# Weighting the first half of the positions in four groups of 128 instead of three, in a local attention and S4 kernel on one Trainium2 core

## The chip, the core and the metric

The kernel runs on one core of one Trainium2 chip. The core has five engines that work at the same time, each in the order of its own queue: TensorE (PE: matrix products, PEld its weight loads), VectorE (DVE), ScalarE (ACT), GpSimd (POOL) and SyncE (SP, which here only issues transfers). Matrix products land in PSUM, a small accumulator memory of eight banks, and are copied from there to SBUF, the working memory, by ScalarE or VectorE. Transfers between SBUF and the chip's main memory are issued from SP, POOL and ACT. The metric is the time of one execution in microseconds; less is better. Three runs of the kernel before gave 405.63, 408.08 and 410.88 us.

## The reference

Two independent layers read their own inputs, and their outputs stand side by side in one array of 2048 rows and 1280 columns.

```python
# A: attention over 8 positions, 2 apart, 32 heads of 20 dimensions
qkv = (x @ wqkv)                       # x: 2048 x 640
logits[h, s, w] = q[h, s] . k[h, s - 2 w] * 20 ** -0.5     # w = 0..7, -1e9 where s - 2 w < 0
attn = softmax(logits over w)
o[h, s] = sum over w of attn[h, s, w] * v[h, s - 2 w]
a = o @ wo
# B: state-space layer, as a long convolution
K[d, l] = Re(sum over n of C * exp(dt * A * l) * dt * B)   # 640 x 192 states, l < 2048
y = irfft(rfft(u padded) * rfft(K padded)) + u * Dskip     # along the 2048 positions
out = concat(a, y)
```

## The kernel before

Layer B is computed first: the kernel K from tables of exponentials and sines, then transforms along the positions as matrix products. Its spectra go to main memory (Zdram, UDdram) and come back at the end for the last inverse step. Layer A's projections of keys and queries, its logits and the first softmax lie between and behind these. The change touches only the last stage, from about 317 us of the profiled execution on.

The 2048 positions are held as four segments of 512 (one per 32 partitions: partition 32 s + h is head h of segment s). "First half" means positions 0 to 255 of each segment, "second half" positions 256 to 511; each half has its own softmax (arguments 0 and 1 of `softmax_a`, `exp`, `sums`, `reciprocal`, `softmax_b`). The first half's weights are ready before the stage begins; the second half's softmax is finished inside it.

**Values.** `proj_v(d)` projects two of the 20 value dimensions, d and d+1, for all positions: 40 matrix products into one two-bank PSUM buffer, and one copy by ScalarE into the tile v. There are three such two-bank buffers, shared by everything that asks for one ("big"). In front of its 512 positions each segment has a halo of 14 columns, the last 14 of the segment before; `v_halo(d0, nd)` fills it for nd dimensions with four small products and one ScalarE copy. It reads the copied v.

**Weighting.** `av_step(i0, ni, j0, nj, w)` is one step: VectorE multiplies the values of 4 nj dimensions at ni positions, shifted by 2 w, by the weights of offset w, into one of six ring buffers (the profile calls them atp and prod); TensorE adds the result over w with 16 matrix products of 32x32 tiles (weights: ident) into two two-bank PSUM buffers ps_o. For w = 0 the shift is zero and no halo column is read. A group is the eight steps w = 0 to 7; at its end two ScalarE copies empty the two buffers. A step's number is n = 8 group + w. A ring buffer is written again six steps later, when its products are done; all groups behind the second use the same two PSUM buffers.

**Pieces.** When the positions of a group have all 20 dimensions, they can be multiplied by wo and sent out: `out_piece`, 10 matrix products of 320 columns, copies (two of 320 columns for the even pieces, one of 640 for the odd ones) and the transfers to the output. There are 16 pieces, numbered here 0 to 15 in order: 0 to 3 and 4 to 7 of the first half, 8 to 10, 11 to 13, and 14 and 15 of the second. From piece 11 on half of a piece's transfers are issued from ScalarE's own queue. `rest` is the list of pieces that may run.

**Parts.** Layer B's last inverse step is 24 parts (`part`), three for each of eight blocks of output rows: a few matrix products, one ScalarE copy (ysb), and after every third part four transfers to the output. Parts 0 to 5 read quarter 0 of the spectra, 6 to 11 quarter 1, 12 to 17 quarter 2, 18 to 23 quarter 3. Quarter 2 is loaded into the space of x (which `proj_v` reads), quarter 3 into the space of quarter 0; `LOADS` issues them at n = 2 to 6 and 8 to 12, 15 transfers of 128 KB for a quarter.

**Order.** A planner orders each engine's queue by which instruction can go first; but from `att.in_order()` on, the stage's matrix products, the copies, the VectorE steps and the output transfers of the pieces are pinned to the order in which the program writes them. `FILLS` is the table that places pieces and parts: n: (pieces, parts), run behind step n (in group 0 the parts run ahead of the step). What is left runs behind the last step.

Of the kernel before, what the change touches and what calls it, by code (L numbers as in the profile page):

```python
# [781 lines left out]
def body(tc, ctx, pools, prm, B_u, B_Dskip, Sd, Zd, UDd, A_x, A_wqkv, A_wo, out_a, out_b):  # L782
# [41 lines left out]
    att = Attention(tc, pools, A_x, A_wqkv, A_wo, out_a, psk, psg)  # L824
# [139 lines left out]
    for w in range(W):  # L964
        if w >= 2:
            att.products(1, w)
        att.logits(1, w)
        att.proj_v(2 * w)
        if w == 4:
            att.v_halo(0, 8)  # L970
    att.in_order()
    inv.open_rows()
    inv.load(1)
# [1 line left out]
    rest = []  # L975

    def fill(some, n=1):
        for f in some[0:n]:
            f()
        del some[0:n]  # L980

    att.open_out(a2)
    GROUPS = ((0, 256, 0, 2, ()), (0, 128, 2, 3, [(s, 1, 0, 128) for s in range(4)]), (128, 128, 2, 3, [(s, 1, 128, 128) for s in range(4)]),
              (256, 96, 0, 5, [(0, 4, i, 32) for i in (256, 288, 320)]), (352, 96, 0, 5, [(0, 4, i, 32) for i in (352, 384, 416)]), (448, 64, 0, 5, [(s, 2, 448, 64) for s in (0, 2)]))
    FILLS = {1: (0, 1), 3: (0, 1), 5: (0, 2), 7: (0, 2), 11: (0, 2), 13: (0, 1), 15: (0, 2), 16: (0, 1), 17: (1, 0), 19: (2, 2), 23: (1, 2), 27: (2, 2), 31: (2, 2), 35: (2, 2), 37: (0, 2), 39: (1, 0), 43: (1, 0), 45: (1, 0)}
    LOADS = {(2, 8)[n // NCH] + n % NCH: (2 + n // NCH, n % NCH) for n in range(2 * NCH)}
    for group, (i0, ni, j0, nj, done) in enumerate(GROUPS):
        for w in range(W):
            n = 8 * group + w
            if group == 0:  # L990
                if w < 7:
                    fill(parts, FILLS.get(n, (0, 0))[1])
                if w == 3:
                    att.exp(1)
                if w in (0, 3):
                    att.proj_v(16 + 2 * (w == 3))
                if w == 5:
                    att.v_halo(8, 12)
            att.av_step(i0, ni, j0, nj, w, group == 5)
            if n in LOADS:  # L1000
                qr, c = LOADS[n]
                inv.load(qr, c, c + 1)
            if n in (9, 11, 13, 14):
                k = (9, 11, 13, 14).index(n)
                att.sums(1, 2 * k, 2 * k + 2)
            if n == 2:
                att.softmax_a(1)
            if n == 17:
                att.reciprocal(1)
                att.softmax_b(1)  # L1010
            if n > 6 and n in FILLS:
                fill(rest, FILLS[n][0])
                fill(parts, FILLS[n][1])
        rest += att.out_proj(done, group == 5)
    for f in parts + rest:
        f()

# [2 lines left out]
def kernel(  # L1020
# [28 lines left out]
    Zd = dpool.tile([NCH, 128, 4096], bf16, name="Zdram")  # L1049
    UDd = dpool.tile([NCH, 128, 2048], bf16, name="UDdram")  # L1050
    body(tc, ctx, pools, prm, B_u, B_Dskip, Sd, Zd, UDd, A_x, A_wqkv, A_wo, out_a, out_b)


# [28 lines left out]
```

## Time and profile before

| | |
|---|---|
| time, median of three runs | 408.08 us (405.63 to 410.88) |
| span of the profiled execution | 400.1 us |
| VectorE busy | 363.8 us (91% of the span) |
| TensorE busy | 345.0 us (86%) |
| ScalarE busy | 308.4 us (77%) |
| weighting steps on VectorE | 335.64 to 387.89 us, 48 steps |
| last matrix product to the end of the span | 395.9 to 400.1 us |

The span runs from the first to the last instruction of one profiled execution; the times of runs also hold what lies around it, 8.0 us at the median. Rows of the timeline have the start in us, the duration in us, the engine, the line of the code, the operation, what it writes and reads, and in square brackets the idle time of the engine just before and what ended it. Several like instructions that follow each other are merged into one row with their count (x4), and its duration goes from the first one's start to the last one's end; neighbouring instructions of an engine overlap by about 0.1 us, so that the time from one start to the next is a little less than the duration. In the stage of the change the helper functions of lines 474 and 475 issue all matrix products and copies, so rows are told apart by their tiles.

### The profile page before, as it was taken

What the parts mean: (1) busy time and instruction counts of PE and PEld (TensorE: products, weight loads), DVE (VectorE), ACT (ScalarE), POOL (GpSimd) and SP (SyncE); (2) the same over time, 40 slices, a digit from 0 to 9 for tenths busy, and PEclk for the clock granted to TensorE, in tenths of its full rate; (3) what the DMA queues carried; (4) which work ended last, traced back from release to release, by engine and by line L of the source; (5) the groups of instructions that cost most, each with busy time, mean ns of one, the idle gap of its engine ahead of it and who ended that gap; (6) DMA issues with size and microseconds to landing.
All of it is one profiled execution on the core that took longest, in us unless ns stands there. A gap on an engine that the chain in (4) does not pass through costs nothing.

```text
span 400.1 us, 18758 instructions
## 1 busy us (share of the span) xinstructions
PE 345.0 (86%) x8565; PEld 258.7 (65%) x8565; DVE 363.8 (91%) x353; ACT 308.4 (77%) x536; POOL 53.5 (13%) x110
## 2 busy tenths in 40 slices
PE   1269779989998798987899999999989999888994
PEld 0157668878886677866788666656765687434652
DVE  8999998997999999979999799997967899999971
ACT  4968999889999899989999775534697554855662
POOL 8472000000010000000001000100001030032230
PEclk9997868999989899999998999999999999989999
DMA  7699103032035001440029544300563173697752
GB/s 171 155 218 188 26 3 134 31 77 61 32 136 121 14 5 57 136 106 3 3 67 206 117 100 120 100 20 3 198 177 110 52 196 78 191 238 217 232 153 81
DMA packets 41840, 43.36 MB, mean 108 GB/s; under 512 B 25409, under 2 KB 35233, under 8 KB 41121
## 3 DMA queue, kind: packets, MB, share of 16 engines
q1 hardware_dynamic: 36656, 30.19, 31.2%
q0 software_dynamic: 4208, 11.43, 9.7%
q8 instruction: 67, 1.10, 1.1%
q10 hardware_dynamic: 896, 0.54, 0.5%
q14 instruction: 13, 0.10, 0.1%
HBM read 19.70 MB, written 14.16 MB: 85 GB/s over the span
## 4 chain that ended last, share of the span: by engine, by line
PE 46%; ACT 37%; DVE 10%; issue 3%; DMA 2%; SPq 1%; ACTq 0%; DVEq 0%
ACT R L252 10%; ACT A L381 8%; ACT A L388 6%; PE ps_ph L289 5%; PE ps_q L558 5%; PE ps_k L540 4%; PE ps_k L366 4%; PE ps_k L361 4%; PE ps_v L571 4%; PE ps_f L387 3%; PE ps_x L474 3%; ACT Z L429 3%; PE ps_o L474 2%; PE ps_ia L428 2%; PE ps_l L602 2%
## 5 line engine op out<-in xcount | busy, mean ns | idle before, releaser
L348 DVE TENSOR_TENSOR Y<-PG 128x3072 bf16<-128x3072 bf16 x60 | 102.9, 1753 | 4.4 <-PE ps_k L366 4.4
L252 ACT ACTIVATE R<-LPB 128x192 bf16<-128x192 f32 (+1 forms) x185 | 56.9, 415 | 0.1
L361 PE MATMUL ps_k<-Y,X 128*32 128x64 bf16 x1920 | 47.0, 239 | 8.5 <-issue 4.2
L361 PEld LDWEIGHTS <-X 128*32 128x32 bf16 x1920 | 32.5, 117 | 18.5 <-issue 9.5
L366 PE MATMUL ps_k<-Y,X 64*32 64x64 bf16 x1920 | 42.9, 233 | 0.1
L388 ACT CAST A<-ps_f 128x1024 bf16<-128x1024 f32 x40 | 37.7, 1045 | 6.5 <-PE ps_f L387 6.5
L289 PE MATMUL ps_ph<-LPB,LPA 128*64 128x256 bf16 x320 | 33.6, 313 | 8.8 <-DMA LPA<-lo 6.6
L381 ACT CAST A<-ps_f 128x1024 bf16<-128x1024 f32 x40 | 37.7, 1031 | 2.3 <-PE ps_f L380 2.3
L318 DVE TENSOR_TENSOR X<-R,TX 128x1536 bf16<-128x1536 bf16 x40 | 37.5, 958 | 0.0
L387 PE MATMUL ps_f<-A,T 128*64 128x128 bf16 x640 | 29.7, 262 | 9.0 <-ACT A L381 8.8
L366 PEld LDWEIGHTS <-X 64*32 64x32 bf16 x1920 | 29.5, 112 | 8.4 <-issue 0.7
L387 PEld LDWEIGHTS <-T 128*64 128x64 bf16 x640 | 27.8, 132 | 10.7 <-issue 10.0
L297 ACT ACTIVATE TA<-ps_ph 128x768 bf16<-128x768 int16 x40 | 29.7, 819 | 3.6 <-PE ps_ph L293 3.5
L681 DVE TENSOR_TENSOR prod<-v,atp 128x1536 bf16<-128x1536 bf16 (+3 forms) x32 | 31.0, 1024 | 1.0 <-ACT v L475 0.5
L297 ACT ACTIVATE TX<-ps_ph 128x768 bf16<-128x768 int16 x40 | 29.7, 840 | 0.3 <-PE ps_ph L293 0.2
L591 DVE TENSOR_TENSOR prod<-qT,kT 128x1024 bf16<-128x1024 bf16 (+1 forms) x16 | 22.9, 1484 | 4.2 <-ACT qT L559 4.2
L289 PEld LDWEIGHTS <-LPA 128*64 128x64 bf16 x320 | 17.5, 122 | 13.0 <-issue 9.3
L540 PE MATMUL ps_k<-xT,wkq 128*128 128x512 bf16 x100 | 22.9, 379 | 0.2 <-ACT A L388 0.2
L293 PE MATMUL ps_ph<-LPB,LPA 128*64 128x128 bf16 x320 | 23.0, 241 | 0.0
L558 PE MATMUL ps_q<-xT,wkq 128*128 128x512 bf16 x100 | 22.6, 379 | 0.0
L318 DVE TENSOR_TENSOR PG<-R,TA 128x3072 bf16<-128x3072 bf16 x10 | 17.5, 1754 | 5.0 <-ACT TA L297 5.0
L380 PE MATMUL ps_f<-BD,U 128*64 128x128 bf16 x320 | 20.5, 286 | 0.8 <-ACT Z L429 0.6
(157 smaller groups left out, 688.5 us busy)
## 6 DMA issues: line engine op xcount, KB each, us to landing
P<-A SPq DMA_DIRECT2D x16, 256.0 KB, 3.0
Zdram<-Z SPq DMA_DIRECT2D x16, 256.0 KB, 2.4
Z<-Zdram SPq DMA_DIRECT2D x30, 128.0 KB, 4.0
U<-in_B_u_dram SPq DMA_DIRECT2D x4, 640.0 KB, 10.6
UDdram<-UD POOLq DMA_DIRECT2D x10, 256.0 KB, 3.1
out_dram<-ysb SPq DMA_DIRECT2D x32, 80.0 KB, 3.2
Z<-UDdram SPq DMA_DIRECT2D x16, 128.0 KB, 4.1
Z<-Zdram POOLq DMA_DIRECT2D x10, 128.0 KB, 5.9
```

The costliest lines, as they stand in the source:

```text
L252: exp = lambda o, i, m: nc.scalar.activation(out=o, in_=i, func=ACT.Exp, scale=m)
L289: MM(o[64 * hh:64 * hh + 64, :, 0:8], lhsT=L[:, 64 * hh:64 * hh + 64], rhs=rhs, start=first, stop=last, skip_group_check=True, tile_positi ...
L297: last = nc.scalar.activation(out=dst, in_=words.rearrange("p b (q e f) -> p b q (e f)", e=8, f=4), func=ACT.Sin, scale=PI_LO / 32768.0)
L318: TT = lambda o, a, b, op: V.tensor_tensor(out=o, in0=a, in1=b, op=op)
L348: nc.vector.tensor_tensor(out=Y[:].rearrange("p q (b a) f -> p q b a f", a=8), in0=fa, in1=gb, op=A.mult)
L361: MM(ps[32 * g:32 * g + 32, t], lhsT=X[:, q, k, :, f], rhs=Ys[k][:, q, :, f], start=(t == 0 and k == 0), stop=False, tile_position=(0, 32 ...
L366: MM(ps[32 * g:32 * g + 32, t], lhsT=X[hb, q, k, :, f], rhs=Ys[k][hb, q, :, f], start=False, stop=(k == 2), tile_position=(64 * (g // 2), ...
L381: nc.scalar.copy(out=A1[:, 8 * b:8 * b + 8], in_=ps[:])
L387: last = MM(ps[sl, kk], lhsT=C["T2"][:, 8 * b + kk, sl], rhs=A1[:, :, 8 * b + kk, :], start=(kk % 4 == 0), stop=True, skip_group_check=Tru ...
L388: nc.scalar.copy(out=A1[:, :, 8 * b:8 * b + 8, :], in_=ps[:].rearrange("p k (j g) -> p j k g", g=4))
L540: MM(ps[:, i], lhsT=self.wk[:, kt, 128 * ct:128 * ct + 128], rhs=self.x4[:, kt, 2 * i:2 * i + 2, 256 * hf:256 * hf + 256], start=(kt == 0) ...
L558: MM(ps[:, i], lhsT=self.wq[:, kt, 128 * ct:128 * ct + 128], rhs=self.x4[:, kt, 2 * i:2 * i + 2, 256 * hf:256 * hf + 256], start=(kt == 0) ...
```

## The change

The first half of the positions is weighted in four groups of eight steps instead of three, and the placing of the work around is rewritten:

- groups: 0 to 127 with dimensions 0 to 11, 0 to 127 with 12 to 19, 128 to 255 with 0 to 11, 128 to 255 with 12 to 19, where it was 0 to 255 with dimensions 0 to 7, then 0 to 127 and 128 to 255 with 8 to 19 each. The second half's three groups stay. There are 56 steps in place of 48; pieces 0 to 3 can run behind step 15 as before, 4 to 7 behind step 31 (it was 23), 8 to 10 behind 39 (31), 11 to 13 behind 47 (39);
- `proj_v(18)` goes ahead of step 1 instead of step 3; the halo is filled for dimensions 0 to 7, 8 to 11 (new, behind `proj_v(12)`) and 12 to 19 (ahead of step 3) in place of 0 to 7 and 8 to 19 (ahead of step 5);
- `FILLS` is new, and the sums of the second half's softmax are at steps 11 to 14 instead of 9, 11, 13, 14. `LOADS` and the steps behind which `softmax_a(1)`, `reciprocal(1)` and `softmax_b(1)` run (2 and 17) keep their numbers.

```diff
@@ -966,8 +966,8 @@
         att.logits(1, w)
         att.proj_v(2 * w)
-        if w == 4:
-            att.v_halo(0, 8)
+        if w in (4, 6):
+            att.v_halo(*((0, 8), (8, 4))[w // 6])
     att.in_order()
@@ -980,9 +980,11 @@
     att.open_out(a2)
-    GROUPS = ((0, 256, 0, 2, ()), (0, 128, 2, 3, [(s, 1, 0, 128) for s in range(4)]), (128, 128, 2, 3, [(s, 1, 128, 128) for s in range(4)]),
+    GROUPS = ((0, 128, 0, 3, ()), (0, 128, 3, 2, [(s, 1, 0, 128) for s in range(4)]), (128, 128, 0, 3, ()), (128, 128, 3, 2, [(s, 1, 128, 128) for s in range(4)]),
               (256, 96, 0, 5, [(0, 4, i, 32) for i in (256, 288, 320)]), (352, 96, 0, 5, [(0, 4, i, 32) for i in (352, 384, 416)]), (448, 64, 0, 5, [(s, 2, 448, 64) for s in (0, 2)]))
-    FILLS = {1: (0, 1), 3: (0, 1), 5: (0, 2), 7: (0, 2), 11: (0, 2), 13: (0, 1), 15: (0, 2), 16: (0, 1), 17: (1, 0), 19: (2, 2), 23: (1, 2), 27: (2, 2), 31: (2, 2), 35: (2, 2), 37: (0, 2), 39: (1, 0), 43: (1, 0), 45: (1, 0)}
+    END = len(GROUPS) - 1
+    FILLS = {3: (0, 1), 4: (0, 1), 5: (0, 1), 6: (0, 2), 9: (0, 2), 11: (0, 1), 15: (0, 1), 17: (1, 1), 18: (0, 1), 19: (1, 1), 21: (1, 1), 23: (1, 1), 27: (0, 2), 31: (0, 2),
+             33: (1, 0), 35: (1, 1), 37: (1, 1), 39: (1, 1), 41: (1, 1), 43: (1, 1), 45: (1, 1), 49: (1, 0), 51: (1, 0), 53: (1, 0)}
     LOADS = {(2, 8)[n // NCH] + n % NCH: (2 + n // NCH, n % NCH) for n in range(2 * NCH)}
@@ -992,16 +994,16 @@
                 if w == 3:
                     att.exp(1)
-                if w in (0, 3):
-                    att.proj_v(16 + 2 * (w == 3))
-                if w == 5:
-                    att.v_halo(8, 12)
-            att.av_step(i0, ni, j0, nj, w, group == 5)
+                if w in (0, 1):
+                    att.proj_v(16 + 2 * w)
+                if w == 3:
+                    att.v_halo(12, 8)
+            att.av_step(i0, ni, j0, nj, w, group == END)
...
-            if n in (9, 11, 13, 14):
-                k = (9, 11, 13, 14).index(n)
+            if n in (11, 12, 13, 14):
+                k = n - 11
                 att.sums(1, 2 * k, 2 * k + 2)
...
-        rest += att.out_proj(done, group == 5)
+        rest += att.out_proj(done, group == END)
     for f in parts + rest:
         f()
```

## The prediction

> **What bounds the kernel now.** I read the busy times first, then the stretches of the last stage, then VectorE's timeline there.
>
> ```profile
> PE 345.0 (86%) x8565; PEld 258.7 (65%) x8565; DVE 363.8 (91%) x353; ACT 308.4 (77%) x536; POOL 53.5 (13%) x110
> ```
>
> ```profile
> core 0: us, PE busy (x) PEld busy (x) DVE busy (x) ACT busy (x) POOL busy (x), PEclk, DMA share, GB/s
> 336.00:347.30 11.30, 10.75 (x260) 6.33 (x253) 10.69 (x12) 7.42 (x9) 0.00 (x0) 1.00 0.46 140
> ...
> 388.00:400.10 12.10, 6.92 (x106) 4.05 (x104) 1.87 (x4) 3.65 (x8) 0.00 (x0) 1.00 0.35 98
> ```
>
> No engine is the bound alone: VectorE is full from 336 to 388, TensorE nearly so (10.75 of 11.30 us in the second row), and the last 12 us belong to neither. VectorE's rows in order of time:
>
> ```profile
> 311.12 1.83 DVE L591 TENSOR_TENSOR prod<-qT,kT 128x1024 bf16<-128x1024 bf16 x3
> ...
> 335.64 2.36 DVE L681 TENSOR_TENSOR atp<-v,atp 128x2048 bf16<-128x2048 bf16 x2
> ...
> 339.05 0.42 DVE L615 TENSOR_TENSOR soft<-soft,lsb 128x512 bf16<-128x512 bf16 x1
> ...
> 340.98 3.49 DVE L681 TENSOR_TENSOR prod<-v,atp 128x2048 bf16<-128x2048 bf16 x3
> 344.38 2.35 DVE L681 TENSOR_TENSOR atp<-v,atp 128x2048 bf16<-128x2048 bf16 x2
> 347.28 3.69 DVE L681 TENSOR_TENSOR prod<-v,atp 128x1536 bf16<-128x1536 bf16 x4 [0.54 <-ACT v L475]
> ...
> 352.62 3.56 DVE L681 TENSOR_TENSOR prod<-v,atp 128x1536 bf16<-128x1536 bf16 x4
> 356.09 1.75 DVE L639 RECIPROCAL soft<-ps_x 128x256 bf16<-128x256 f32 x1
> ...
> 359.02 1.82 DVE L681 TENSOR_TENSOR atp<-v,atp 128x1536 bf16<-128x1536 bf16 x2
> ...
> 364.23 2.22 DVE L681 TENSOR_TENSOR atp<-v,atp 128x1920 bf16<-128x1920 bf16 x2
> ...
> 386.33 1.56 DVE L681 TENSOR_TENSOR prod<-v,atp 128x1280 bf16<-128x1280 bf16 x2 [0.31 <-PE ps_o L474]
> ```
>
> The first half takes VectorE from 335.64 to 364.23, and 0.54 us of that is waiting, for the copy of the last two value dimensions. The last step ends at 387.89, and then the chain of waits runs through TensorE (start, length, what):
>
> ```profile
> 365.54 0.59 PE ps_ib L474 x12
> 366.13 0.92 PE ps_o L474 x64
> 367.05 1.46 PE ps_x L474 x10
> ...
> 377.67 1.04 PE ps_o L474 x64
> ...
> 390.14 0.42 PE ps_o L474 x32
> 390.56 1.48 PE ps_x L474 x10
> 392.04 0.42 ACT ob L475
> ...
> 392.49 0.50 DVE ob L707
> ...
> 393.04 1.53 PE ps_op L474 x10
> ```
>
> TensorE ends the last step at 390.56, 2.7 us behind VectorE, runs piece 13, and waits for two copies; pieces 14 and 15 start at 393.04. What starts at 393.04 is the same after the change, so the forecast is where that start moves.
>
> **VectorE's work.** From one start to the next a step takes 3.40/3 = 1.13 us with 2048 elements (340.98 to 344.38) and 3.47/4 = 0.87 with 1536 (352.62 to 356.09): 0.52 ns an element and 0.07 us for each instruction. A step of 1024 isn't in the trace; by that line it takes 0.60, and the product of that size (first row) 1.83/3 = 0.61 at most. The first half had 8 x 1.13 + 16 x 0.87 = 23.0 us and gets 16 x 0.87 + 16 x 0.60 = 23.5: **+0.5 us**.
>
> **The values' wait.** This is the larger term. Rows of ScalarE, then of TensorE:
>
> ```profile
> 337.10 1.01 ACT L573 CAST v<-ps_v 128x1024 bf16<-128x1024 f32 x1 [1.69 <-PE ps_v L571]
> ...
> 341.96 1.01 ACT L475 CAST v<-ps_v 128x1024 bf16<-128x1024 f32 x1 [1.15 <-PE ps_v L474]
> 343.11 0.56 ACT L475 CAST ysb<-ps_ib 128x480 bf16<-128x480 f32 x1
> ...
> 344.43 1.91 ACT L626 ACTIVATE lsb<-lsb 128x2048 bf16<-128x2048 bf16 x1
> ...
> 347.93 0.31 ACT L475 CAST v<-ps_h 128x168 bf16<-128x168 f32 x1
> ...
> 354.91 1.50 ACT L475 CAST o<-ps_o 128x768 bf16<-128x768 f32 x2 [0.72 <-PE ps_o L474]
> ...
> 374.29 1.82 ACT L475 CAST ob<-ps_o 128x960 bf16<-128x960 f32 x2
> ...
> 390.84 1.15 ACTq L731 DMA_DIRECT2D out_dram<-ob  x2
> ```
>
> ```profile
> 334.71 2.33 PE L571 MATMUL ps_v<-xT,wv 128*32 128x512 bf16 x40
> 336.87 0.72 PE L602 MATMUL ps_l<-prod,wv 128*32 128x256 bf16 x20
> ...
> 341.84 0.43 PE L474 MATMUL ps_o<-atp,ident 32*32 32x512 bf16 x16
> ...
> 357.79 2.65 PE L474 MATMUL ps_op<-wo,o 128*128 128x320 bf16 x10
> ```
>
> TensorE projects values without a gap until 341.84 (2.16 us a projection, 334.71 to 336.87), while VectorE already weights. Step 0 needs no halo, so with dimensions 0 to 11 it starts at 335.64 still. Step 1 needs the halo of dimensions 8 to 11. It comes behind `proj_v(12)`, at 336.87 on TensorE, and behind that projection's copy on ScalarE (337.10 + 1.01), so at 338.35: VectorE idles from 336.51, 1.8 us, where before it had work. The new halo's products and copy cost about 0.15 and 0.3 us; ScalarE has 1.1 to 1.7 us free between the projections' copies.
>
> The rest of the values come no earlier. `proj_v(18)` now follows `proj_v(16)` with one step between, and of the three two-bank buffers group 0 holds two; the third is freed by the copy 341.96 + 1.01 = 342.97. So: projection 342.97 to 345.13, copy to 346.15, in the pinned order the copy of part 0 (0.5) to 346.65, the exponential to 348.5, the last halo's copy to 348.8. VectorE has by then done eight steps (6.9), the second softmax's maximum and difference (339.05 to 340.98: 1.93) and step 8 (0.6), is there at 347.0, and idles again 1.8 us before step 9. From 348.8 it has 7 x 0.60 + 8 x 0.87 + 8 x 0.60 for steps 9 to 31, and the reciprocal and the scaling (356.09 to 359.02: 2.93): 18.9, so **367.7** for step 32's start, against 364.23.
>
> Removing the order's knot alone (the halo's copy ahead of the exponential) would not save it all: parts 1 to 4 and the two copies of group 0 (four times 0.5, 1.5) keep ScalarE until 352, TensorE can't put step 8 into the buffers before, and the ring stops VectorE at step 14. I add **0.4** for that.
>
> **Quarter 2.** In the chain's first row part 12 starts at 365.54, when a transfer lands; I read that as its spectra. SP issues the same transfers in the same order; I take the same landing. Part 12 stands behind step 21 now; VectorE ends that at 361.5, and TensorE is through it and piece 2 at 363.6, so it waits too. From 365.54: part 12 (0.27; parts have 0.20 to 0.27 each, 0.59 for x12 being two), steps 22 and 23 (0.23 each, 0.92/4), piece 3 (1.46), part 13 (0.26), step 24 (0.19: 0.23 with 384 columns and 0.21 with 320, 0.42/2, leave little less for 256): 368.2. Step 30 waits for step 24's ring buffer; steps 30 and 31 end at 369.4, TensorE's step 31 at 370.0. Had the quarter come by 362, VectorE would be there at 368.1.
>
> **TensorE from there.** Two copies of 512 elements (0.55, as 0.75 for 768 and 0.9 for 960 give) empty the buffers by 371.2; step 32 is done at 371.4. Steps 33 to 40 with pieces 4 to 7 and parts 18 to 20: 8 x 0.26 (1.04/4) + 4 x 1.46 + 0.73 = 8.65, and 0.6 of short waits for VectorE and copies: 380.65. Steps 41 to 47 with pieces 8 to 10 and parts 21 to 23: 1.82 + 4.38 + 0.73: 387.6. Behind step 47 FILLS has nothing, where piece 10 stood behind that group's last step (39) before; the copies of 960 elements (1.82) lie bare: step 48 is done at 389.7. Steps 49 to 55 with pieces 11 to 13: 7 x 0.21 + 4.38 = 5.85: **395.55**. Before, TensorE ended its last step at 390.56 with piece 13 still to run. That piece no longer follows, but its copy (0.65 from 395.15) and its two issues (1.15) stand in ScalarE's queue ahead of the last copies, as piece 12's did (390.84 to 391.99): 396.9, then 0.42 and 0.50 as in the chain: pieces 14 and 15 at **397.8**.
>
> Work that has cover: 128 more matrix products, in the 0.19 above; moved sums, done on TensorE by 355.1, just ahead of the reciprocal at 355.2. Quarter 3's transfers wait for part 5, the last reader of their space, now behind step 9 instead of 7. Rows of POOL and of SP's queue:
>
> ```profile
> 349.38 1.10 POOL L758 DMA_DIRECT2D Z<-Zdram  x2 [22.22 <-DMA Z<-Zdram]
> ```
>
> ```profile
> 370.95 0.59 SPq L758 DMA_DIRECT2D Z<-UDdram  x1
> ```
>
> POOL's seven would start at 352.4 instead of 349.38, early enough. SP's eight stand behind quarter 2's as before; the last was issued at 370.95, and part 18 comes at 375.5 (371.4, steps 33 to 35, pieces 4 and 5, 0.4 of waits): 4 us for it to land, a thin cover, priced below.
>
> **Sum.** 397.8 - 393.04 = +4.8. The span becomes 400.1 + 4.8 = 404.9; with the 8.0 around it that the median of 408.08 has over the span, **412.9 us** (+1.2%).
>
> **Rivals.** *The first half is recovered.* The four first pieces can run 4.3 us of VectorE's work earlier (8 x 1.13 + 8 x 0.87 against 8 x 0.87 + 8 x 0.60), so TensorE no longer drags 4.7 us behind at the half (step 24's products at 367.05 + 1.46 + 0.46 for two parts = 369.0, against 364.23), and one piece leaves the tail. For this to decide, both values' waits must vanish or stay under about 1 us together, by an order of projections other than the text's. Then step 32 starts at 364.23 + 0.5, TensorE follows VectorE through two groups of 8 x 1.07 (to 381.9), the bare copies and step 48's wait take 2.4, the last group 8 x 0.21 + 4.38, and the way to pieces 14 and 15 2.2 as above: 392.6, so 407.6 us. For it: TensorE's projections ahead of the pinned stretch may be reordered. Against: it is full there, 10.75 of 11.30 us. 0.17.
>
> *The clock falls at the wrong place.* One stretch ran at a lower granted clock (0.54, in the column before the DMA share):
>
> ```profile
> 355.60:357.80 2.20, 1.58 (x37) 0.58 (x36) 2.20 (x2) 2.11 (x5) 0.00 (x0) 0.75 1.06 231
> 357.80:360.30 2.50, 2.50 (x26) 1.30 (x10) 2.47 (x4) 0.48 (x2) 0.00 (x0) 0.54 0.93 247
> ```
>
> There ten products took 2.65 us instead of the chain's 1.48, with no harm, as VectorE had work. TensorE will idle more at 347 to 352 (1.7 us where part 2 waits for the last halo's copy to free its PSUM bank, 1.0 at step 8), so the drop may come at 352 to 355, on the 3 us of steps and sums that the reciprocal waits for: +2 for VectorE, of which quarter 2's wait hides 1.3 and the rest with slower pieces gives 1 to 2 more: 414.5. The Trainium skill (TensorE: Matmul & The Clock Gate, "What's actually happening") says that the clock halves only after an idle window of about 3.4 us; by that rule idle times of 1.7 us change nothing, and the sum stays 412.9. The second row agrees with the half speed; the first doesn't fit the window, since TensorE was busy 1.58 of 2.20 us there and the clock was already falling. 0.13.
>
> *Spectra later.* If POOL's later transfers crowd SP's last ones of quarter 2 and quarter 3 by 2.5 to 3.5 us, every time from 365.54 or 375.5 on moves by 2.4 to 3.6: 415.3 to 416.5. 0.12.
>
> The forecast with its near neighbours (411 to 414) has 0.58. **Range** 407.5 to 416.8: from the recovered case to the late spectra. Two per cent, 8.2 us, is about what a measurement of this kernel can tell from no change. Over 416.2 lies the upper end of the third rival and what I haven't thought of: 0.12. Below 399.9 nothing named leads: VectorE had only 0.85 us of waits to win from 336 to 388, and the tail 3 at most; 0.02. Within: 0.86.
>
> **What will show it.** VectorE idle 1.8 us before steps 1 and 9 (released by ScalarE's v), the last halo's copy at 348.8; step 32 at 368 to 369.4; bare copies of 960 elements before step 48; piece 13 ahead of the last step, and pieces 14 and 15 at 397.8. The forecast is wrong if step 9 starts before 347.5, or if TensorE is done with step 55 before 393.

## Result and profile after

The changed kernel takes 416.89 us (median of 6 runs, 414.75 to 419.34), the kernel before 406.75 beside it (6 runs, 404.71 to 410.88): a ratio of 1.0257, 95% interval 1.0211 to 1.0303, or some 10 us more. The forecast was 412.9, range 407.5 to 416.8. The direction was right; the size was twice the forecast's +4.8, and the time lies just above the range. Here and below, the ratios leave out executions over 1.5% above the fastest of the same kernel, so they can differ a little from the ratio of two medians.

The profiled execution has a span of 417.1 us and took 418.86. That leaves 1.8 us around the span, not the 8.0 that the prediction used. Its baseline, the span of 400.1, therefore belongs to an execution of about 401.9 us, some 4 us under the median of the 78 executions of the kernel before that were measured with the experiments below (405.9; one of 675.20 us is left out). Step 0 starts at 339.32, 3.7 us later than in the profile of before. That offset arises ahead of the changed code (step 0 starts anywhere from 334.8 to 340.2 in these profiles, in either kernel), so the times below are counted from step 0.

The page's first row, and then VectorE's timeline (start, length, instructions; in brackets the idle time ahead and what ended it):

```profile
PE 356.3 (85%) x8697; PEld 259.6 (62%) x8697; DVE 365.2 (88%) x361; ACT 309.4 (74%) x539; POOL 54.9 (13%) x110
```

```profile
339.32 0.95 DVE L681 TENSOR_TENSOR atp<-v,atp 128x1536 bf16<-128x1536 bf16 x1
341.92 0.96 DVE L681 TENSOR_TENSOR atp<-v,atp 128x1536 bf16<-128x1536 bf16 x1 [1.65 <-ACT v L585]
...
353.18 1.90 DVE L681 TENSOR_TENSOR prod<-v,atp 128x1024 bf16<-128x1024 bf16 x3 [1.87 <-ACT v L475]
...
361.78 1.76 DVE L639 RECIPROCAL soft<-ps_x 128x256 bf16<-128x256 f32 x1 [2.09 <-PE ps_x L474]
...
373.21 1.29 DVE L681 TENSOR_TENSOR prod<-v,atp 128x1024 bf16<-128x1024 bf16 x2 [0.79 <-PE ps_o L474]
375.42 1.29 DVE L681 TENSOR_TENSOR atp<-v,atp 128x1024 bf16<-128x1024 bf16 x2 [0.91 <-PE ps_o L474]
376.63 4.36 DVE L681 TENSOR_TENSOR prod<-v,atp 128x1920 bf16<-128x1920 bf16 x4
```

VectorE did 1.4 us more work (365.2 against 363.8) and waits in new places. The two waits released by ScalarE's `v` stand ahead of steps 1 and 9, 1.65 and 1.87 us long, as forecast (1.8 and 1.8). The third, 2.09 us ahead of the reciprocal, was not in the sum; it is released by TensorE's sums. Step 32 starts at 376.63, which is 37.3 us after step 0, where the forecast had 32.1 without and 33.8 with the wait for quarter 2.

What made the sums late shows in the stretches of the trace (length, then busy time of PE, PEld, DVE, ACT and POOL with counts, the granted clock, and the DMA's share and rate):

```profile
355.00:358.40 3.40, 2.48 (x72) 0.65 (x65) 3.11 (x6) 2.58 (x5) 1.10 (x3) 0.50 0.45 132
358.40:361.90 3.50, 3.50 (x79) 1.10 (x78) 1.41 (x3) 0.56 (x1) 2.71 (x5) 0.50 0.88 207
361.90:365.30 3.40, 3.10 (x57) 1.23 (x42) 3.37 (x3) 1.40 (x3) 0.00 (x0) 0.50 0.98 325
365.30:368.60 3.30, 3.30 (x51) 1.14 (x48) 3.30 (x5) 1.54 (x4) 0.57 (x1) 0.50 0.75 186
...
378.90:382.30 3.40, 3.40 (x50) 1.24 (x47) 3.40 (x4) 1.82 (x4) 0.00 (x0) 0.50 0.53 130
...
409.60:413.00 3.40, 3.29 (x13) 1.51 (x11) 0.56 (x2) 0.58 (x2) 0.00 (x0) 0.50 0.18 48
```

From 355.0 to 368.6 TensorE has half its clock, 13.6 us without a break, from 15.7 to 29.3 us after step 0. The profile of before had 3.4 us of it there (the 0.54 row). Two further stretches of 3.4 us lie behind step 32 and on the last two pieces. TensorE's rows, and two of ScalarE's, show the rest:

```profile
357.90 0.61 PE L474 MATMUL ps_x<-lsb,ident 128*128 128x256 bf16 x2
...
378.56 0.30 PE L474 MATMUL ps_o<-atp,ident 32*32 32x256 bf16 x9 [1.48 <-issue]
...
398.83 0.33 PE L474 MATMUL ps_o<-atp,ident 32*32 32x320 bf16 x8 [1.05 <-ACT ob L475]
399.69 0.46 PE L474 MATMUL ps_o<-atp,ident 32*32 32x320 bf16 x24 [0.53 <-ACT ob L475]
...
405.32 0.49 PE L474 MATMUL ps_o<-atp,ident 32*32 32x320 bf16 x32
408.44 1.79 PE L474 MATMUL ps_op<-wo,ob 128*128 128x320 bf16 x10 [2.63 <-DVE ob L707]
410.02 1.54 PE L474 MATMUL ps_x<-wo,ob 128*128 128x320 bf16 x5
411.36 1.54 PE L474 MATMUL ps_o<-wo,ob 128*128 128x320 bf16 x5
```

```profile
406.15 1.24 ACTq L731 DMA_DIRECT2D out_dram<-ob  x2
407.43 0.75 ACT L475 CAST ob<-ps_o 128x320 bf16<-128x320 f32 x2 [1.31 <-issue]
```

Two sums take 0.61 us at half clock (0.39 in the run warm below, at full clock). Ahead of step 48 TensorE waits 1.05 and 0.53 us for the bare copies, as forecast. Piece 13's two issues stand ahead of the last copies on ScalarE, as forecast. TensorE ends step 55 at 405.81, 66.5 us after step 0 (forecast 59.9), and the last two pieces start at 408.44 and take 4.5 us (until 412.90), with half the clock under them.

### The profile page after: what moved, and what is told of

Its sections match the earlier page's. It is cut to its first block, busy times and chain, and to the rows that moved or that the text cites. A ratio compares the mean times of both kernels' runs of the same rounds, so it can differ in the third digit from the quotient of the medians.

```text
span 417.1 us, 19041 instructions
## 1 busy us (share of the span) xinstructions
PE 356.3 (85%) x8697; PEld 259.6 (62%) x8697; DVE 365.2 (88%) x361; ACT 309.4 (74%) x539; POOL 54.9 (13%) x110
## 5 line engine op out<-in xcount | busy, mean ns | idle before, releaser
L361 PE MATMUL ps_k<-Y,X 128*32 128x64 bf16 x1920 | 47.7, 239 | 10.2 <-issue 8.1
L361 PEld LDWEIGHTS <-X 128*32 128x32 bf16 x1920 | 32.1, 117 | 21.2 <-issue 12.6
L318 DVE TENSOR_TENSOR X<-R,TX 128x1536 bf16<-128x1536 bf16 x40 | 37.4, 956 | 0.0
L681 DVE TENSOR_TENSOR prod<-v,atp 128x1920 bf16<-128x1920 bf16 (+3 forms) x36 | 31.7, 930 | 3.8 <-ACT v L475 1.9
L297 ACT ACTIVATE TX<-ps_ph 128x768 bf16<-128x768 int16 x40 | 29.9, 828 | 2.1 <-PE ps_ph L293 1.2
L293 PE MATMUL ps_ph<-LPB,LPA 128*64 128x128 bf16 x320 | 23.2, 241 | 0.0
L380 PE MATMUL ps_f<-BD,U 128*64 128x128 bf16 x320 | 20.4, 283 | 0.8 <-ACT Z L429 0.6
```

The source lines that it names most:

```text
L293: MM(o[64 * hh:64 * hh + 64, :, 8:12], lhsT=L[:, 128:192], rhs=rhs[:, :, 16 * hh:16 * hh + 16], start=False, stop=last, skip_group_check=T ...
L297: last = nc.scalar.activation(out=dst, in_=words.rearrange("p b (q e f) -> p b q (e f)", e=8, f=4), func=ACT.Sin, scale=PI_LO / 32768.0)
L318: TT = lambda o, a, b, op: V.tensor_tensor(out=o, in0=a, in1=b, op=op)
L361: MM(ps[32 * g:32 * g + 32, t], lhsT=X[:, q, k, :, f], rhs=Ys[k][:, q, :, f], start=(t == 0 and k == 0), stop=False, tile_position=(0, 32 ...
L681: ins = nc.vector.tensor_tensor(out=p2.rearrange("p (d i) -> p d i", i=ni), in0=self.v2[:, 4 * j0:4 * j0 + 4 * nj, off:off + ni], in1=at[: ...
```

## Experiments

Ratios are to the kernel before on the same chip, with 95% intervals. The table gives, for each profile, the start of the second softmax's reciprocal and of the second half's first step (step 24 or 32) in us after step 0, and the half-clock stretches up to the second half's first step and behind it, without those behind TensorE's last product; beside them the ratio of all its runs.

| kernel | reciprocal | second half | half clock to there / behind | ratio |
|---|---|---|---|---|
| before | 20.5 | 28.6 | 3.4 / 0 | 1 |
| before_again | 20.4 | 28.6 | 3.4 / 6.8 | - |
| before_third | 20.6 | 28.7 | 10.2 / 0 | - |
| after | 22.5 | 37.3 | 13.6 / 6.8 | 1.0257 |
| after_again | 22.4 | 37.4 | 13.7 / 10.2 | - |
| values_only | 23.2 | 31.3 | 17.1 / 0 | 0.999 |
| warm | 20.6 | 35.2 | 0 / 3.4 | 1.0162 |
| halo_first | 22.3 | 36.3 | 10.2 / 6.8 | 1.0259 |
| cover47 | 22.5 | 37.5 | 13.6 / 0 | 1.0181 |
| warm_cover | 20.5 | 33.6 | 0 / 0 | 1.0109 |
| cold_halo | 23.5 | 37.5 | 13.6 / 3.4 | 1.0196 |
| warm_halo | 21.3 | 34.4 | 0 / 3.4 | 1.0097 |
| warm_early | 21.4 | 35.4 | 0 / 3.4 | 1.0113 |

**The same kernels again.**

> The kernel after, for a second profile. Clock theory: again 10 us or more at half speed from about step 8 on, and VectorE idle about 2 us before the reciprocal. Wait theory: 1.8 us idle before steps 1 and 9 in every execution, while the length of the half-speed stretch varies and the time doesn't follow it.

> The kernel before, for a second profile. Clock theory (the granted clock falls where TensorE idles in the first half, and that is most of the loss): TensorE at half speed for one stretch of about 3.4 us behind 350, as in the first profile, or for none; time 404 to 411. Wait theory (VectorE waits for values and sums whatever the clock does): the same rows whatever the clock shows.

> The kernel before, for a third profile, to see what of its last stage repeats. Expected: 28.6 us from step 0 to step 24 with one half-speed stretch of 3.4 us behind step 16, in line with the two profiles so far; the 3.9 us wait of the second profile (TensorE waiting 4.65 us for a transfer before part 12) comes and goes.

The changed kernel took 416.6 us and had the same waits of VectorE (1.65, 0.60, 1.84 and 2.09) and the same long stretch. The kernel before took 410.73 and 407.53. From step 0 to the second half it repeats to 0.1 us. Of the 8.9 and 5.6 us by which their spans exceed the 400.1 of the profile before, 3.1 and 3.6 arise ahead of step 0, and the rest behind the second half's start: in the first of the two, part 12 waits for a transfer.

```profile
371.83 0.99 PE L474 MATMUL ps_ib<-Z,HB 96*32 96x480 bf16 x12 [4.65 <-DMA out_dram<-ysb]
```

That is 33.1 us after step 0, where the prediction's row had 29.9 (365.54). The row names an output transfer, but the instruction waits for several, and the one that landed just ahead of it, at 371.78, is the last load of quarter 2 (at 365.49 in the profile of before). So an execution of the kernel before can lose some 4 us on quarter 2. This one is 5 us over the median; before_third waited 0.71 us there, and the profile that the forecast was built on 1.44. before_third also has 10.2 us at half clock, but from 19.0 us after step 0 on, too late to delay the reciprocal at 20.6: the place counts, not the length alone.

**The clock.** Products with a tile of zeros, added to the accumulators, fill the gaps of TensorE ahead of the drop; nothing else changes.

```diff
+        self.zero = a2.tile([128, 128], bf16, name="zero")
+        nc.gpsimd.memset(self.zero[:], 0.0)
...
+            if (i0, j0, w, sc) == (0, 3, 0, 2):
+                self.warm(8, 256)
...
+    def warm(self, k, n):
+
+        for _ in range(k):
+            self.MM(self.ops[0][:, 0, 0:n], lhsT=self.zero[:], rhs=self.wo[:, 0, 0:n], start=False, stop=False, skip_group_check=True)
...
+                if w == 5:
+                    att.warm(7, 384)
...
+                if w == 1:
+                    att.warm(5, 384)
                 if w in (0, 1):
                     att.proj_v(16 + 2 * w)
```

> The kernel after with 20 matrix products of zero weights (128x128, 256 or 384 columns) put where TensorE waited: ahead of the projection of dimensions 18 and 19, of part 2 and of the second half of step 8. They add zero to sums in progress. Clock theory: the clock stays at 1.0 through 350 to 370, the reciprocal's 2.1 us of waiting goes, and the time falls by 4 to 7 us, to a ratio of 1.008 to 1.016 to before. Wait theory: the products fill idle time only, the time stays within 1 us of 416.9.

411.67 us, 1.0162 (1.0076 to 1.0248). VectorE's timeline:

```profile
348.74 1.90 DVE L683 TENSOR_TENSOR prod<-v,atp 128x1024 bf16<-128x1024 bf16 x3 [1.87 <-ACT v L475]
...
355.39 1.76 DVE L639 RECIPROCAL soft<-ps_x 128x256 bf16<-128x256 f32 x1 [0.45 <-PE ps_x L474]
...
368.82 1.29 DVE L683 TENSOR_TENSOR atp<-v,atp 128x1024 bf16<-128x1024 bf16 x2 [0.91 <-PE ps_o L474]
```

The wait for the values stays to the hundredth (1.87), the clock stays full up to step 32, and the wait for the sums falls from 2.09 to 0.45. The second half does not follow in full, and TensorE's rows say why:

```profile
365.81 0.39 PE L474 MATMUL ps_ib<-Z,HB 96*32 96x480 bf16 x4 [1.57 <-DMA Z<-Zdram]
```

With TensorE on time, quarter 2's landing (31.0 us after step 0 here) is the next limit. The late TensorE of the changed kernel had hidden it. The landing differs from one execution to the next: in warm_cover and warm_halo part 12 starts 29.4 and 30.2 us after step 0, 0.05 us behind the landing, and TensorE waits 0.1 us or less.

**The placement of the values alone**, in the kernel before, with its own groups:

```diff
-        if w == 4:
-            att.v_halo(0, 8)
+        if w in (4, 6):
+            att.v_halo(*((0, 8), (8, 4))[w // 6])
...
-                if w in (0, 3):
-                    att.proj_v(16 + 2 * (w == 3))
-                if w == 5:
-                    att.v_halo(8, 12)
+                if w in (0, 1):
+                    att.proj_v(16 + 2 * w)
+                if w == 3:
+                    att.v_halo(12, 8)
```

> The kernel before with only the values placed as in the kernel after (dimensions 18 and 19 ahead of step 1, the halo in three fills); groups and FILLS as before. Forecast's reading: step 0 to 7 need the halo of dimensions 0 to 7 only, so step 1 doesn't wait; the last halo comes at about the same time as before, so the time stays within 1 us of before. Clock theory: TensorE idles no more than before, half speed for 3.4 us behind step 16 at most. Either way the loss needs the new groups. A rival reading, that the placing of the values alone costs 4 us or more, falls if the ratio is below 1.006.

406.24 us, 0.999 (0.9941 to 1.0039). Stretches, then VectorE:

```profile
346.30:349.70 3.40, 1.76 (x80) 0.69 (x66) 2.10 (x2) 3.40 (x5) 0.00 (x0) 1.00 0.61 164
349.70:353.10 3.40, 3.34 (x88) 1.23 (x95) 3.36 (x4) 2.16 (x5) 0.21 (x1) 0.50 0.72 217
353.10:366.70 13.60, 13.35 (x236) 4.28 (x213) 11.80 (x14) 6.60 (x13) 3.93 (x8) 0.50 0.75 204
```

```profile
359.42 1.76 DVE L639 RECIPROCAL soft<-ps_x 128x256 bf16<-128x256 f32 x1 [1.77 <-PE ps_x L474]
...
370.75 4.37 DVE L681 TENSOR_TENSOR prod<-v,atp 128x1920 bf16<-128x1920 bf16 x4 [0.96 <-PE ps_o L474]
```

Half the clock for 17 us and a late reciprocal, and no loss: the second half starts 2.7 us late (31.3 against 28.6), but TensorE then has no wait for quarter 2, which costs the kernel before 0.7 to 4.7 us in its profiles. The placement brings the long stretch by itself; the loss needs the new groups too, where VectorE is late already.

**The knot in the order.** The last halo ahead of the exponential:

```diff
-                if w == 3:
-                    att.exp(1)
                 if w in (0, 1):
                     att.proj_v(16 + 2 * w)
                 if w == 3:
                     att.v_halo(12, 8)
+                    att.exp(1)
```

> The kernel after with the last halo's copy put ahead of the exponential on ScalarE. Forecast's reading: step 9 no longer waits (1.9 us), but the ring stops VectorE five steps later, so 0 to 0.5 us are gained. Clock theory: part 2 no longer waits 1.25 us for the halo's PSUM bank, so TensorE idles less and the clock may hold: 4 us or more gained where it does. Wait theory: the 1.9 us come back in full.

415.27 us, 1.0259 (1.0173 to 1.0346): nothing. The wait ahead of step 9 goes, 1.45 us of it come back ahead of step 12, and the reciprocal waits 2.09 as before.

**The bare copies.** One fill, piece 10, moves from behind step 45 to behind step 47 (some of the recorded expectations speak of two), and with it TensorE has work under the copies; warm_cover has the zero products too.

```diff
-             ... 45: (1, 1), 49: (1, 0), 51: (1, 0), 53: (1, 0)}
+             ... 45: (0, 1), 47: (1, 0), 49: (1, 0), 51: (1, 0), 53: (1, 0)}
```

> The kernel after with piece 10 moved from behind step 45 to behind step 47, so that the two copies of 960 elements have a matrix product beside them. Forecast's sum: 1.5 to 1.8 us gained (the bare copies), from 416.9 to about 415. Clock theory: the gap is also what makes the clock fall in the last stretch of some executions, so 1.5 to 4 us are gained; the half-speed stretch from step 8 on stays.

> The products of zero weights and piece 10 behind step 47 together. Clock theory: no half-speed stretch in the stage, time 1.5 to 4 us under that of the zero products alone (411.7 beside 404.8 for before), so a ratio of 1.005 to 1.013. Wait theory: the same as the kernel with piece 10 moved alone.

413.59 us, 1.0181 (1.0103 to 1.0259), and 411.48, 1.0109 (1.0054 to 1.0164). In warm_cover's profile no stretch of the stage has half clock. TensorE there:

```profile
391.24 0.46 PE L474 MATMUL ps_o<-atp,ident 32*32 32x320 bf16 x24 [0.18 <-ACT ob L475]
...
396.87 0.49 PE L474 MATMUL ps_o<-atp,ident 32*32 32x320 bf16 x32
400.52 1.53 PE L474 MATMUL ps_op<-wo,ob 128*128 128x320 bf16 x10 [3.16 <-DVE ob L716]
401.89 0.84 PE L474 MATMUL ps_x<-wo,ob 128*128 128x320 bf16 x5
402.57 0.84 PE L474 MATMUL ps_o<-wo,ob 128*128 128x320 bf16 x5
```

The waits ahead of step 48 fall to 0.18, and the last pieces take 2.9 us (400.52 to 403.41). Piece 13's copy and issues still keep the last copies waiting (3.16).

**A piece more behind step 41 in the kernel before**, so that no piece is left behind its last step:

```diff
-             ... 39: (1, 0), 43: (1, 0), 45: (1, 0)}
+             ... 39: (1, 0), 41: (1, 0), 43: (1, 0), 45: (1, 0)}
```

> The kernel before with piece 13 moved from behind the last step to behind step 41, so that its tail is ordered as in the kernel after. The forecast's step: TensorE's last step ends one piece later, and the piece's copy and two issues stand ahead of the last copies, so pieces 14 and 15 start about 1 us later or at the same time; no gain. The other reading, that one piece less behind the last step shortens the tail, gives 1 to 1.5 us less.

408.29 us, 1.0067 (1.0017 to 1.0117). A piece run ahead of the last step instead of behind it gains nothing: its copy and issues then stand ahead of the last copies, and TensorE waits 2.23 us for these, where it waited 1.01 in the profile of before.

**More room for the values.** parts_late has halo_first's edit and moves parts 1 to 4 behind steps 9 and 11 (the next ones follow later, so that eight parts instead of nine stand ahead of the reciprocal); mended also fills the halo of dimensions 8 to 11 ahead of `proj_v(12)` and covers step 47; mended_warm has zero products as well (5 of 384 columns, 16 of 256).

```diff
-    FILLS = {3: (0, 1), 4: (0, 1), 5: (0, 1), 6: (0, 2), 9: (0, 2), 11: (0, 1), 15: (0, 1), ...
-             33: (1, 0), 35: (1, 1), ...
+    FILLS = {3: (0, 1), 9: (0, 2), 11: (0, 2), 13: (0, 1), 15: (0, 2), ...
+             33: (1, 1), 35: (1, 1), ...
```

> The kernel after with the last halo's copy ahead of the exponential and parts 1 to 4 moved from steps 4 to 6 to behind steps 9 and 11 (later ones follow). ScalarE reaches the two copies of group 0 about 2 us earlier. Forecast's sum: the wait before step 9 and the ring's wait both shrink, step 32 comes 1.5 to 2.5 us earlier. Clock theory: TensorE has less work between 346 and 355, and the half-speed stretch stays, so the reciprocal still waits 1.5 to 2 us and little is gained (under 1.5 us); if the shorter gaps keep the clock up, 4 us or more.

> The kernel after with all its waits for values mended: the halo of dimensions 8 to 11 ahead of the projection of 12 and 13, the last halo's copy ahead of the exponential, parts 1 to 4 behind steps 9 and 11, and piece 10 behind step 47. Forecast's sum: the waits before steps 1 and 9 go (1.65 and 1.87), step 32 at 28.6 + 0.5 + 0.6 + what the clock takes (2.5, the wait before the reciprocal) = 32 us from step 0, and the tail as with piece 10 moved: ratio 1.006 to 1.013. If the groups themselves cost more (ring, PSUM, more steps), it stays at 1.018.

> The same with 21 products of zero weights where TensorE waits (ahead of the projection of 18 and 19, and in step 8). Clock theory: no half-speed stretch in the first half, the reciprocal's wait of about 2.5 us falls under 0.5, 1 to 3 us gained against the mended kernel without them: ratio 1.000 to 1.008. If the lower clock is a bystander, the two mended kernels are equal.

417.36 us, 1.0289 (1.0219 to 1.0358); 415.27, 1.0268 (1.0214 to 1.0322); 414.54, 1.0258 (1.0213 to 1.0304). Step 32 comes earlier in all three (34.9, 34.2 and 33.7 us after step 0), and nothing of it reaches the end. A row of ScalarE in mended:

```profile
374.28 1.46 ACT L475 CAST ysb<-ps_ib 128x480 bf16<-128x480 f32 x3 [1.29 <-DMA out_dram<-ysb]
```

Later parts give their rows to SP behind quarter 3's loads, so the `ysb` buffers come free late, ScalarE waits for one, and TensorE for ScalarE. These kernels moved too much at once to tell what the values' waits are worth.

**The values' waits alone**, with piece 10 behind step 47 and without moving a part. All three fill the halo of dimensions 8 to 11 ahead of `proj_v(12)`; cold_halo and warm_halo have the last halo ahead of the exponential too; the warm ones have warm's zero products.

```diff
+        if w == 6:
+            att.v_halo(8, 4)
         att.proj_v(2 * w)
-        if w in (4, 6):
-            att.v_halo(*((0, 8), (8, 4))[w // 6])
+        if w == 4:
+            att.v_halo(0, 8)
```

> The changed kernel with the zero products, the two fills behind step 47, the halo of dimensions 8 to 11 computed ahead of proj_v(12), and the last halo ahead of the exponential; no part is moved. With the zero products and the cover alone VectorE's waits ahead of the second half add up to 4.55 us (1.65 before step 1, 0.66, 1.84 before step 9, 0.40 before the reciprocal), the first half's own work is 0.5 longer, and step 32 starts 33.64 us after step 0 where the kernel before has 28.59. Theory (what is left of the loss is these waits, as the prediction's own terms have it): the first wait falls to 0.4 or less, the one before step 9 turns into one of about 1.4 before step 12, step 32 starts 31.5 to 32.5 us after step 0, and the time falls from 1.011 of the kernel before to about 1.006 (409). Rival (what is left sits behind step 32, in the tail): step 32 starts earlier, and the time stays at 1.011 or above.

> The same two moves of halos, with the two fills behind step 47 and without the zero products. With the fills alone the ratio was 1.018 and step 32 started 37.5 us after step 0, with 13.6 us at half speed. Theory (half speed decides, the values' waits are hidden below it): TensorE stays at half speed from about step 8 on, step 32 starts no earlier than 36, and the ratio stays at 1.016 to 1.02. Rival (the waits are what takes the speed away, so that TensorE stays at full speed without them): less than 7 us at half speed ahead of step 32, which starts by 34, and a ratio near 1.010.

> The zero products, the fills behind step 47 and only the halo of dimensions 8 to 11 ahead of proj_v(12); the last halo stays behind the exponential. Theory: the wait before step 1 goes (1.65), the one before step 9 takes it up in part, since the last halo's copy comes no earlier: it grows from 1.84 to 3 or more, step 32 starts 33.2 to 33.7 us after step 0, and the ratio stays at 1.010 to 1.012. Rival (each wait counts for itself): step 32 at 32.0 and a ratio of 1.007.

410.96 us, 1.0097 (1.0057 to 1.0137); 414.57, 1.0196 (1.0148 to 1.0244); 410.67, 1.0113 (1.0077 to 1.0149). VectorE in warm_halo:

```profile
338.89 0.43 DVE L615 TENSOR_TENSOR soft<-soft,lsb 128x512 bf16<-128x512 bf16 x1 [1.23 <-ACT lsb L605]
...
346.13 0.96 DVE L683 TENSOR_TENSOR atp<-v,atp 128x1536 bf16<-128x1536 bf16 x1 [1.76 <-PE ps_o L474]
...
350.25 0.69 DVE L683 TENSOR_TENSOR prod<-v,atp 128x1024 bf16<-128x1024 bf16 x1 [1.11 <-PE ps_o L474]
...
356.25 1.76 DVE L639 RECIPROCAL soft<-ps_x 128x256 bf16<-128x256 f32 x1 [0.55 <-PE ps_x L474]
```

Both waits for values are gone, and 5.1 us of others stand in their place (these four, and 0.24 and 0.19 more): for the logits' copy, for ring buffers that TensorE has not emptied, for the sums. With warm_cover they were 4.6 (1.65, 0.66, 1.84, 0.40). The expectation of 1.006 fell. In warm_early the wait ahead of step 9 stays 1.84, the other waits grow (1.22, 1.76, 0.69), and TensorE waits 0.84 us for quarter 2; the time is the same. cold_halo and warm_halo, measured side by side, differ by the zero products alone, and their intervals do not touch: half clock costs about 4 us, and it comes without the values' waits as well.

**The order of the groups.** warm_swap exchanges groups 1 and 2, so that the last eight dimensions are wanted 7 us later; cold_swap does it without zero products. Both have the halo of dimensions 8 to 11 ahead of `proj_v(12)` and piece 10 behind step 47. In recip_late (cover47 besides) the reciprocal stands behind step 23.

```diff
-    GROUPS = ((0, 128, 0, 3, ()), (0, 128, 3, 2, ...), (128, 128, 0, 3, ()), (128, 128, 3, 2, ...),
+    GROUPS = ((0, 128, 0, 3, ()), (128, 128, 0, 3, ()), (0, 128, 3, 2, ...), (128, 128, 3, 2, ...),
...
-    ... 17: (1, 1), 18: (0, 1), 19: (1, 1), 21: (1, 1), 23: (1, 1), 27: (0, 2), 31: (0, 2),
+    ... 17: (0, 1), 18: (0, 1), 19: (0, 1), 21: (0, 1), 23: (0, 1), 25: (1, 0), 27: (1, 2), 29: (1, 0), 31: (1, 2),
```

> The kernel with the zero products, the fills behind step 47 and the halo of dimensions 8 to 11 ahead of proj_v(12), in which the first half's groups also change places: twelve dimensions of positions 0 to 127, twelve of 128 to 255, then eight of each, so that the last two dimensions are wanted 7.0 us of VectorE's work later; the four pieces of the first positions move from steps 17 to 23 to steps 25 to 31. Theory (the waits come from too little work ahead of fixed dates: 7.0 + 1.9 us of work stand ahead of the last halo's copy where the kernel before had 9.1 + 1.9, and 13.6 us of steps ahead of the reciprocal where it had 17.8): the wait for the last halo (1.84) goes, those ahead of the reciprocal add up to 3 or less, step 32 starts 31.3 to 33 us after step 0 against 35.4 without the exchange; of that the four pieces, which now come eight steps later, may take back up to 3 in the tail: a ratio of 1.000 to 1.010. Rival (the waits are those of a TensorE that is full until step 15, whatever VectorE has to do): VectorE waits at the ring instead, 4 us or more in all, step 32 at 34 or later, a ratio of 1.011 or above.

> The same exchange of groups without the zero products. Theory of the clock (half speed comes from TensorE's gaps while only steps and sums are left for it): 7 us or more at half speed ahead of step 32, step 32 between 33 and 36, a ratio of 1.008 to 1.016. Rival (with the first wait and the last halo's wait gone TensorE keeps its speed): less than 4 us at half speed there, and the ratio of the kernel with zero products.

> The changed kernel with the two fills behind step 47, and the second softmax's reciprocal and scaling behind step 23 in place of step 17; only step 32 needs them. With the fills alone the ratio was 1.018 and step 32 started 37.5 us after step 0, 2.1 us of it a wait for the sums. Theory (the half speed costs time through the sums, which come 2 us later while VectorE stands at the reciprocal): the wait goes, step 32 starts at 35.0 to 35.8, and the ratio falls to about 1.013. Rival (TensorE at half speed is the bound of the whole stretch, the sums only show it): VectorE waits as long at the ring of the steps, step 32 stays at 37, and the ratio at 1.018.

417.06 us, 1.0287 (1.0225 to 1.0349); 415.41, 1.0264 (1.0207 to 1.032); 417.08, 1.03 (1.0251 to 1.0349). In warm_swap the reciprocal starts 21.6 us after step 0, with 4.1 us of waits ahead of it, 1.76 of them at the ring ahead of step 7: work that needs no late values does not bring it forward. Then quarter 2 is waited for, and step 32 comes at 36.8.

```profile
366.82 0.59 PE L474 MATMUL ps_ib<-Z,HB 96*32 96x480 bf16 x4 [3.06 <-DMA Z<-Zdram]
```

Half clock runs from 23.5 to 37.1 us after step 0 there in spite of the zero products (in cold_swap from 15.5 to 39.4), so the time behind the reciprocal tells nothing clean. recip_late tells nothing either: the sums lie in the PSUM buffer that pieces use from step 19 on, so its reciprocal is taken of other numbers and waits 4.85 us for a piece's copy.

## Why the prediction was wrong in size

**Right.** The values' waits (1.65 and 1.87, forecast 1.8 each), the last halo's copy as the cause of the second (13.8 us after step 0, forecast 13.2), the bare copies ahead of step 48, and piece 13's copy and issues ahead of the last copies. The first half was not recovered. Quarter 2's landing does set part 12's start where TensorE is on time (29.4, 30.2 and 31.0 in warm_cover, warm_halo and warm, forecast 29.9); the rival of later spectra did not decide, since the changed kernel's late TensorE waits for no transfer behind step 9. With the clock full and step 47 covered, TensorE ended step 55 59.3 us after step 0 and pieces 14 and 15 started at 62.5 (396.87 + 0.49 and 400.52, less 338.03), where the forecast had 59.9 and 62.2. That the two agree so closely is in part luck: the forecast's times hold some 2 us of bare copies, which this kernel does not have.

**The step that failed** is the clock. Sum and steps stood on full-clock rows, and the rival "the clock falls at the wrong place" was given 0.13 and a price of 1 to 2 us, for one drop at 352 to 355. The drop came nearly where it said (15.7 us after step 0, where 352 to 355 was 16.4 to 19.4; on the sums that the reciprocal waits for, with +2 for VectorE), but it lasted 13.6 us, and more 3.4 us stretches followed behind later gaps. From the profiles, against the forecast: step 32 comes 3.5 us later than 33.8; from there to the end of step 55 it takes 29.2 us in place of 26.2, with a stop of 1.48 and a half-clock stretch in it; the wait ahead of the last two pieces is 0.4 longer, and the pieces take 4.5 in place of 2.9. From the ratios: the zero products are worth 0.0095, 0.0072 and 0.0099 of the time in three pairs (after and warm, cover47 and warm_cover, cold_halo and warm_halo), 3 to 4 us. Only the last pair's intervals are apart. In two more pairs they gained nothing (mended and mended_warm 0.0010, cold_swap and warm_swap -0.0023); there they took away only some 7 and 5 us of an execution's half-clock time, by the sum of the next paragraph, and 15 to 18 us in the first three.

The pooled clock agrees with it. From time and mean clock, the half-clock time of an execution is 2 x (1 - clock) x time: 36 us in 78 executions of the kernel before, 52 in 7 of the changed one, 33 to 35 in warm, warm_cover, warm_early and warm_halo. The place counts here too: values_only has 41 and loses nothing.

**Mis-sized beside it.** The forecast's bare copies were worth about 2 (387.6 to 389.7); covering step 47 was worth 0.0076 and 0.0053 (after and cover47, warm and warm_cover), 2 to 3 us, with intervals that overlap. What is left with both gone, 1.0097 to 1.0113 or 4 to 4.6 us, stands against the rest of the forecast's sum (4.8 less 2). It is somewhat larger, and its cause fits only in part: the prediction put it on the order of projections, halo and exponential, and these can be undone without gain. A reading that fits the profiles: the reciprocal's date belongs to TensorE, 20.4 to 21.6 us after step 0 where the clock stays full, or falls late, and no part is moved (19.6 in mended_warm, which has one part less ahead of it), and by that date VectorE has now done 18 steps of 13.6 us, where it had 18 of 17.8 (8 x 1.13 + 10 x 0.87 against 8 x 0.87 + 8 x 0.60 + 2 x 0.87). The 4.2 us are left for later, and show as 3.7 to 5.5 us of waits ahead of the reciprocal in the six kernels with zero products, wherever these fall. That moving the waits does not gain is shown; that the date is TensorE's throughput, and not one wait that no run removed, is argued. Where the 4 us reach the end of the span stays open.

**The base.** The 8.0 us added to the span held 1.8 us around it and 6.2 by which that one execution lay under the median then shown. The latter is the same for both kernels only if both lose as much in an ordinary execution. In before_again and before_third some 3 us of it arise ahead of step 0, where the change touches almost nothing; the rest arises behind the second half's start, with quarter 2 landing 33.1 and 31.9 us after step 0 (29.9 in the profile before) and, in before_again, 6.8 us of half clock behind it, just what the change alters.

**Open:** the stop released by "issue" in steps 30 to 32 (0.25 to 2.8 us in ten of the profiles with four groups, in none with three), for which the profile shows no wait. The traces point to TensorE's own instructions: in all ten the stop stands behind the 16321st record of TensorE (weight loads and the entries of its own queue counted), whatever work comes next, and ends 1.3 to 1.7 us after a transfer of 16 KB of the kind "instruction" (queue 8) has landed. In the profile of before the next record starts 3.6 us after such a landing, without a stop. No run varied it. No version tried beats the kernel before.

## What to carry to other kernels

Where VectorE and TensorE run in step, smaller steps save more on VectorE than on TensorE (0.87 to 0.60 us a step against 0.24 to 0.20, in warm_early), and less of VectorE's work then stands ahead of every date that TensorE sets: count the work done by that date. Here, removing single waits for values only moved them. In these kernels a stretch of small products with gaps of 1 to 2 us on TensorE had a second price, half its clock for some multiple of 3.4 us, which counted only where its next result was waited for; cheap products in the gap told whether that was the case. Before a forecast stands on one profile, ask by how much that execution lies under the median, and why.

## What was not expected of the hardware

The granted clock was 1.0 or 0.5 and nothing between, in stretches of 3.4 us and multiples of it; the 0.75 and 0.54 of the prediction's rows are averages over both. The drop needs no idle stretch: TensorE was busy 1.76 of 3.40 us just ahead of it in values_only, and in the changed kernel

```profile
351.60:355.00 3.40, 2.15 (x92) 1.00 0.69 203
```

(TensorE's busy time, clock, DMA). It kept its clock in warm_cover with 3.39 and 3.40 of 3.40 busy. But no share of busy time decides it: the kernel before kept its clock behind a window with less,

```profile
363.50:366.90 3.40, 1.96 (x81) 1.06 (x78) 3.30 (x4) 1.69 (x4) 1.10 (x2) 1.00 0.77 236
366.90:370.30 3.40, 3.40 (x101) 2.00 (x86) 3.40 (x4) 3.10 (x6) 0.54 (x1) 1.00 0.68 197
```

and in before_again the clock fell at 210.0 us, with TensorE busy the whole 3.40 us ahead. It did fall behind an idle window as well (367.0 to 370.4 in before_again, 0.18 us busy). The Trainium skill (TensorE: Matmul & The Clock Gate, "What's actually happening") puts the drop behind at least one idle window of about 3.4 us; its two levels and its window agree with the trace, but the trace also has drops without that condition, and it was the rule by which the prediction's sum stayed at full clock.

Nor does being busy bring it back: in values_only TensorE was busy 13.35 of 13.60 us, with products of 32x32 tiles and sums, and stayed at half clock. Where the clock was low when the first whole piece began (ten products of 128x128), it was back 1.5 to 5.3 us later (2.3 in before, 4.0 in values_only, 4.6 in after, 5.3 in before_third). That the kind of product decides fits these profiles; no run tried it alone, and the zero products, 128x128 too, fill the gaps and change the kind at once.
